# Batch 0's queries and keys loaded by runs of six rows, batch 2 turned on TensorE, batches 1 and 2 back to back

## The chip, the cores and the metric

The kernel runs on one core of one Trainium2 chip. The metric is device time in microseconds (us) of a whole execution, as the median of several. The span of a profile is about 1.8 us shorter than the time of the same execution, because it runs from the first to the last instruction.

## The reference, cut to what matters

Attention with 16 extra "beacon" keys in front of the causal ones, then a SwiGLU feed-forward block over all tokens.

```python
B, H, S, Nb, D = 8, 8, 576, 16, 64          # 4608 tokens of 512
k_all = concatenate([beacon_k, k], axis=2); v_all = concatenate([beacon_v, v], axis=2)
scores = (1 / sqrt(D)) * q @ k_all.T        # causal mask on the 576 ordinary keys
a = softmax(scores)
x = (a @ v_all).transpose(0, 2, 1, 3).reshape(B * S, H * D)
g = x @ w_gate                              # 512 -> 1536
out = (g * sigmoid(g) * (x @ w_val)) @ w_out
```

## The kernel before

Everything is kept in bf16, with f32 sums in PSUM. Per batch and pair of heads, the kernel multiplies turned (transposed) q by turned k (`S`, scores), takes exponentials on ScalarE, and multiplies by v (`P`). The result x is turned (`X`), and the feed-forward block eats it in chunks of 512 tokens: `G` is a gate unit of 8 products of 128x512 (1.73 us of TensorE at full clock), `F` one of its output products (0.22 us). The order of all these pieces is written by hand as a string, `plan`: each engine runs its part of the string strictly in order. So a piece whose data has not come yet stops TensorE, even where other work would be ready.

Before the scores, q and k must be turned so that D lies on the partitions. Batches 0 and 1 are turned on TensorE (`K`, `Q`: five transposes into a small PSUM bank, then a copy), later batches by DMA transposes (`t`). `l` is one load, issued by GpSimd, which also casts f32 to bf16. Of the other letters, `c` and `d` cast k and q of batch 0, `w` adds four spare turns without a result, `g` is a part of a gate unit, and a small `k`, `q` or `x` is the same turn, copied out by ScalarE.

```python
NPE = 2                                      # batches 0 and 1 are turned on TensorE
...
    def transpose_pair(dst, src, n, b, m, pool, tag, eng):
        t_ps = pool.tile([P, KPAD], BF16, name="t_ps", tag=tag)
        t, h = tiles(src[b % 2]), slice(2 * m, 2 * m + 2)
        while spare:                         # spare turns keep the clock up
            spare.pop()
            nc.tensor.transpose(t_ps[:, 0:P], below[:], ident[:])
        for c in range(NKT):
            r = P if c < 4 else 80
            nc.tensor.transpose(t_ps[:, P * c : P * c + r], t[0:r, c, h, :], ident[0:r, 0:r])
        o, i = dst[b % 2][:, m, 0 : 4 * P + n], t_ps[:, 0 : 4 * P + n]
        ...                                  # copied by ScalarE or VectorE
...
    start = v_loads(0, 0, 4) + q_loads(0, 4, H) + v_loads(0, 4, H)   # 17 issues
    for i in range(4):
        start += w_loads(i)                  # gate and value weights
    start += k_loads(1, 0, H) + q_loads(1, 0, H) + v_loads(1, 0, H)
...
    plan = [
        "lllllllllllllllllllllllllllllllwllllllllllloo",
        "dQwwwwcKdc", "SwwKcwwSwwwQ", "SKPcSQP", "SQKPXSP", "SPXSP",      # batch 0
        "gPgPgxXglgg", "ggGGGGGkKGGkQlGqkGG", "llqll",                   # gates; turns of batch 1
        "lSFFlFSFFFlqttltt", "ltllSFPFSPlllFltFFtFtSt", ...              # batch 1; DMA turns of batch 2
```

The softmax here doesn't subtract the row's maximum and nothing guards it: scores larger than these inputs give would overflow.

Of the kernel before, what the change touches and what calls it, by code (L numbers as in the profile page):

```python
# [8 lines left out]
ACT = mybir.ActivationFunctionType  # L9
ALU = mybir.AluOpType  # L10
BF16 = mybir.dt.bfloat16
FP32 = mybir.dt.float32
# [9 lines left out]
XWRAP, XSHIFT = 5 * TOK, 5 * TOK - P  # L22
XCOLS = XWRAP + P

NPE = 2

NHT = 2

# [23 lines left out]
def kernel(  # L52
# [37 lines left out]
    ident = static.tile([P, P], BF16, name="ident")  # L90
    below = static.tile([P, P], BF16, name="below")

    QK = NKT * H * D
    q32 = static.tile([P, QK // NPAIR * 2], FP32, name="q32")
    k32 = static.tile([P, QK], FP32, name="k32")
    qb = [static.tile([P, QK], BF16, name=f"qb{i}") for i in range(2)]
    kb = [static.tile([P, QK], BF16, name=f"kb{i}") for i in range(2)]
    vb = [static.tile([P, NKT, H, 68], BF16, name=f"vb{i}") for i in range(2)]
    qT = [static.tile([P, NPAIR, KPAD], BF16, name=f"qT{i}") for i in range(2)]
    kT = [static.tile([P, NPAIR, KPAD], BF16, name=f"kT{i}") for i in range(2)]  # L100
# [5 lines left out]


    def tiles(t):
        return t[:].rearrange("p (c h d) -> p c h d", c=NKT, d=D)

    def spans(eng, dst, src, b, h0, h1, c0, c1, r):

        for h in range(h0, h1):
            eng.dma_start(
                dst[:, c0:c1, h, 0:D],
                src[b, h, r : r + P * (c1 - c0), :].rearrange("(c p) d -> p c d", p=P),
            )

    loaded = {}

    def rows(eng, dst, src, b, h0, h1, c, p0, r, n):
# [3 lines left out]
        return eng.dma_start(  # L125
            dst[p0 : p0 + n, c, h0:h1, 0:D], src[b, h0:h1, r : r + n, :].rearrange("h j d -> j h d")
        )

    def load_q_f32(eng, b, h0, h1):
        spans(eng, tiles(q32), q, b, h0, h1, 0, 4, 0)  # L130
        rows(eng, tiles(q32), q, b, h0, h1, 4, 0, 512, 64)

    def load_k_f32(eng, b, h0, h1):
        d = tiles(k32)
        rows(eng, d, k, b, h0, h1, 0, NB, 0, P - NB)
        spans(eng, d, k, b, h0, h1, 1, 4, P - NB)
        rows(eng, d, k, b, h0, h1, 4, 0, 496, 80)

    def q_loads(b, h0, h1):
        d = tiles(qb[b % 2])  # L140
# [17 lines left out]
    def v_loads(b, h0, h1):  # L158
        return key_loads(nc.gpsimd, vb[b % 2], v, beacon_v, b, h0, h1)
# [16 lines left out]

    spare = []

    def cast_k(b, m):
        h = slice(2 * m, 2 * m + 2)  # L180
        nc.vector.tensor_copy(tiles(kb[b % 2])[:, :, h, :], tiles(k32)[:, :, h, :])

    def cast_q(b, m, eng):
        d, t, h = tiles(qb[b % 2]), tiles(q32), slice(2 * m, 2 * m + 2)
        for o, i in ((d[:, 0:4, h, :], t[:, 0:4, h, :]), (d[0:64, 4, h, :], t[0:64, 4, h, :])):
            if eng is nc.scalar:
                nc.scalar.activation(o, i, ACT.Copy)
            else:
                nc.vector.tensor_copy(o, i)

    def copy(eng, o, i):
        if eng is nc.scalar:
# [1 line left out]
        else:  # L194
            nc.vector.tensor_copy(o, i)

    def transpose_pair(dst, src, n, b, m, pool, tag, eng):
        t_ps = pool.tile([P, KPAD], BF16, name="t_ps", tag=tag)
        t, h = tiles(src[b % 2]), slice(2 * m, 2 * m + 2)

        while spare:
            spare.pop()
            nc.tensor.transpose(t_ps[:, 0:P], below[:], ident[:])
        for c in range(NKT):
            r = P if c < 4 else 80
            nc.tensor.transpose(t_ps[:, P * c : P * c + r], t[0:r, c, h, :], ident[0:r, 0:r])
        o, i = dst[b % 2][:, m, 0 : 4 * P + n], t_ps[:, 0 : 4 * P + n]
        if eng is nc.scalar:
            nc.scalar.activation(o, i, ACT.Copy)
        else:  # L210
            nc.vector.tensor_copy(o, i)

    def transpose_k(b, m, pool, tag, eng=None):
        transpose_pair(kT, kb, 80, b, m, pool, tag, eng)

    def transpose_q(b, m, pool, tag, eng=None):
        transpose_pair(qT, qb, 64, b, m, pool, tag, eng)

    def dma_transposes(b):
        def one(dst, src, c, n):  # L220
# [163 lines left out]


    nc.vector.memset(pt[1][:, 0, 0:TOK], 0.0)  # L386
    nc.vector.memset(tiles(k32)[64:P, 4, :, :], 0.0)
    rows(nc.gpsimd, tiles(k32), beacon_k, 0, 0, H, 0, 0, 0, NB)
    make_identity(nc, ident)

    nc.gpsimd.memset(below[:], 0.0)
# [16 lines left out]

    warm(18, TOK)
    for i in range(2):  # L410
        nc.vector.memset(tiles(qb[i])[64:96, 4, :, :], 0.0)
        nc.vector.memset(vb[i][:, :, :, D : D + 1], 1.0)
        nc.vector.memset(vb[i][64:P, 4, :, 0:D], 0.0)
        nc.vector.memset(kT[i][:, :, NB + S : KPAD], 0.0)
        nc.vector.memset(pt[i][:, :, 1664:P_W], 0.0)
    load_k_f32(nc.sync, 0, 0, 2)
    load_q_f32(nc.scalar, 0, 0, 2)
    load_q_f32(nc.scalar, 0, 2, 4)
    for m in range(1, NPAIR):
        load_k_f32(nc.sync, 0, 2 * m, 2 * m + 2)  # L420

    def kq_loads(b):

# [6 lines left out]



    done = dict.fromkeys("SPKQXgGFcdltwo", 0)
    first = [(0, 0, 1), (0, 1, 2), (1, 0, 1), (1, 1, 2), (0, 2, 3), (1, 2, 3), (0, 3, 4), (1, 3, 4)]
    parts = [(j, *part) for j in range(2) for part in first]
    units = [(j, f) for j in range(NCH) for f in range(2 if j < 2 else 0, NF)]
    def free(b, values=False):

        if b < 2 or values:
            return b < 2 or done["P"] >= 8 * (b - 1)  # L440
        return min(done["K"], done["Q"]) >= 4 * (b - 1) if b < 2 + NPE else done["t"] >= 10 * (b - 1 - NPE)

    def v_then(b, h0=0, h1=H):
        return [(load, b, True) for load in v_loads(b, h0, h1)]
# [1 line left out]
    def kq_then(b):  # L446
        return [(load, b, False) for load in kq_loads(b)]

    start = v_loads(0, 0, 4) + q_loads(0, 4, H) + v_loads(0, 4, H)
    for i in range(4):  # L450
        start += w_loads(i)
    start += k_loads(1, 0, H) + q_loads(1, 0, H) + v_loads(1, 0, H)
# [10 lines left out]
        return outp, "outp"  # L463

    def piece(kind):
        n = done[kind.upper()] if kind in "kqx" else done[kind]
        eng = nc.scalar if kind in "kqx" else nc.vector
        if kind == "S":
            b, m = n // 8, n % 8 // 2
            assert done["P"] >= 2 * (n // 2) - 2  # L470
            assert (min(done["K"], done["Q"]) > n // 2) if b < NPE else done["t"] >= 10 * (b - NPE + 1)
            scores(b, m, ("AB", "DC" if b == 0 else "CD")[n % 2])
        elif kind == "P":
            b, m = n // 8, n % 8 // 2
            assert done["S"] >= 2 * (n // 2 + 1)
            pv(b, m, n % 2, *small())
            if b >= NPE and n % 8 == 7:
                x_transpose(b)
        elif kind in "KkQq":
            turn = transpose_k if kind in "Kk" else transpose_q  # L480
            turn(n // 4, n % 4, *small(), eng)
        elif kind in "Xx":
            assert done["P"] >= 2 * (n + 1)
            x_transpose_pair(n // 4, n % 4, *small(), eng)
        elif kind == "g":
            j, f, k0, k1 = parts[n]
            assert done["X"] >= 4 * j + k1
            gv_mm(j, f, k0, k1)
            if k1 == KD:
                gv_act(j, f)  # L490
        elif kind == "G":
            j, f = units[n]
            assert j < NHT or done["F"] >= (j - NHT + 1) * 4 * NF
            assert done["g"] >= 8 * (j + 1) if j < 2 else done["P"] >= 8 * min(j + 1, B)
            gv_unit(j, f)
        elif kind == "F":
            if not projection:
                projection.extend(out_steps(n // (4 * NF), two_banks if done["P"] == 2 * NPAIR * B else one_bank))
            assert done["o"] == 2
            projection.pop(0)()  # L500
        elif kind == "o":
            load_wo(n)
        elif kind == "w":
            spare.extend(range(4))
        elif kind == "c":
            cast_k(0, n)
        elif kind == "d":
            cast_q(0, n, nc.scalar)
        elif kind == "l":
            load, b, values = loads[n]  # L510
            assert free(b, values)
            load()
        elif kind == "t":
            assert done["S"] >= 8 * (n // 10 + NPE - 1)
            turns[n]()
        done[kind.upper() if kind in "kqx" else kind] += 1

    one_bank = [(outp, "outp")]
    two_banks = [(outp, "outp"), (att, "att")]
    plan = [  # L520
        "lllllllllllllllllllllllllllllllwllllllllllloo",
        "dQwwwwcKdc",
        "SwwKcwwSwwwQ",
        "SKPcSQP",
        "SQKPXSP",
        "SPXSP",
        "gPgPgxXglgg",
        "ggGGGGGkKGGkQlGqkGG",
        "llqll",
        "lSFFlFSFFFlqttltt",  # L530
        "ltllSFPFSPlllFltFFtFtSt",
        "FXFPFSFP",
        "SXPFFSl",
        "llllll",
        "llPgtggPXlFFFlPggFFXgFgF",
        "glFSlSFllGFtttlS",
        "tltlllPGSFFlPGGlFFl",
        "ttttSlPtFFSlGPFlFl",
        "SlPFFFSPG",
        "SlPFFSFllFtPtGGFttt",  # L540
        "PSlllFFFFSlllPllGtGtFttt",
        "SFPFFSlGFFPGFG",
        "lFSPFFFFSFlFGllFlPGFGFlFSFF",
        "FllPFSFllFlPGGGFFFtltFFtt",
        "FlSPtFFFSlllPFFFGGFGFFFFFtttt",
        "SltlPFFFSllPFFFGGGFFFFFF",
        "SllPFFFSPFFFGGGFFFFFF",
        "SlllPFFFtSlllPFFGFGGFFFFFFtttt",
        "SlllPFFFSllPFFFGGGFFFFFFttttt",
        "SllPFFFSllPFFFGGGFFFFFF",  # L550
        "SllPFFFSPFFFGGGFFFFFF",
        "SPFFFSPFFFGGGFFFFFFttttt",
        "SPFFFSPFFFGGGFFFFFFttttt",
# [13 lines left out]
    for kind in "".join(plan).replace(" ", ""):  # L567
        piece(kind)
    del done["w"]
    assert done == dict(S=8 * B, P=8 * B, K=8, Q=8, X=8, g=16, G=len(units), F=4 * NF * NCH, c=4, d=2, o=2, l=len(loads), t=len(turns)), done  # L570


# [28 lines left out]
```

## Time and profile before

| | before |
|---|---|
| median time | 391.8 us |
| span of the profile | 390.7 us |
| TensorE busy | 368.9 us (94%) |
| first scores of batch 0 / 1 / 2 | 11.09 / 51.11 / 78.53 us |
| first full gate unit (batch 0 done) | 31.63 us |
| gate and value weights all landed | 34.9 us |

The row below is the DMA view of the kernel before from 2 to 36 us, 40 slices of 0.85 us: the busy share of the DMA engines in tenths (9 is 90% or more), and the GB/s written.

```profile
DMA  9999999999999999997999999999999999999999
GB/s 217 265 224 198 157 219 190 182 189 208 184 202 189 217 113 109 103 42 77 199 198 205 202 203 205 200 221 190 202 203 202 209 198 205 200 205 194 155 154 155
```

Fourteen slices (to 13.9 us) move batch 0's q, k and v at some 200 GB/s. Five slices of 42 to 113 follow, in which the weights have only just been issued (the first at 15.2 us). Then come the weights at 203, and at the end k of batch 1 at 155. The five weak slices are the only room in this row that an earlier issue could fill. They are not rest: the DMA engines are busy in them too, for 90% or more in four of the five, but little is written.

The last piece of weights, in the chain that ended last (issue, us to landing):

```profile
20.33 14.61 DMA wv<-in_moe_w_val_dram
```

### The profile page before, as it was taken

Reading aid. Unit: us, or ns where it says so; the run is one execution under the profiler, and the core shown is the slowest. Engines: PE = TensorE matmul, PEld = TensorE weight load, DVE = VectorE, ACT = ScalarE, POOL = GpSimd, SP = SyncE. Lnnn points to the kernel's source line nnn. Section 1 sums busy time; section 2 is a strip of 40 time slices with the busy share of each in tenths; the row PEclk is TensorE's granted clock in tenths of the full one; section 3 lists DMA queues with packets and bytes.
Section 4 is the critical chain, followed back from the end, with each engine's and each line's share of the span. In section 5 each row is a group of like instructions: output and inputs, shape, how many; then the busy total and the mean of one; then the engine's idle time right before and its main releaser. Section 6 shows DMA issues by size and latency. Waiting matters only on the chain.

```text
span 390.7 us, 7391 instructions
## 1 busy us (share of the span) xinstructions
PE 368.9 (94%) x2857; PEld 181.9 (47%) x2906; DVE 225.3 (58%) x413; ACT 172.4 (44%) x248; POOL 160.3 (41%) x275
## 2 busy tenths in 40 slices
PE   8899988679899999999999999999999999999995
PEld 3664555334454444444444444444445444444442
DVE  3567734625565566666666666666666636575652
ACT  2663577156665555555555555554552212222210
POOL 8946938577759566435653114311110000000000
PEclk9999999969999999999999999999999999999999
DMA  9999999999979999994998157813000211000012
GB/s 165 151 203 174 152 168 139 157 171 156 153 90 166 132 94 155 159 113 43 161 172 102 34 117 109 100 28 89 29 27 29 60 70 39 27 28 29 28 66 97
DMA packets 171364, 40.83 MB, mean 105 GB/s; under 512 B 161072, under 2 KB 166704, under 8 KB 171328
## 3 DMA queue, kind: packets, MB, share of 16 engines
q0 software_dynamic: 113600, 18.28, 68.8%
q1 hardware_dynamic: 55328, 21.48, 27.2%
q10 hardware_dynamic: 2400, 0.59, 0.8%
q8 instruction: 23, 0.38, 0.4%
q14 instruction: 13, 0.11, 0.1%
HBM read 38.27 MB, written 9.44 MB: 122 GB/s over the span
## 4 chain that ended last, share of the span: by engine, by line
PE 76%; DMA 9%; POOL 7%; DVE 3%; ACT 2%; issue 2%; SPq 1%; POOLq 0%; ACTq 0%
PE gv_ps L331 42%; PE o_ps L368 21%; PE pv_ps L286 6%; PE s_ps L241 5%; DMA wv<-in_moe_w_val_dram 4%; POOL vb L125 3%; DMA wo<-in_moe_w_out_dram 3%; DMA qT<-qb 2%; POOL qb L125 2%; ACT p L263 2%; ACT th L344 1%; POOL wg L164 1%; DVE u L346 1%; DVE hT L349 1%; SPq L222 1%
## 5 line engine op out<-in xcount | busy, mean ns | idle before, releaser
L344 ACT ACTIVATE th<-gv_ps 128x512 f32<-128x512 f32 x108 | 64.4, 597 | 164.1 <-PE gv_ps L331 163.4
L346 DVE SCALAR_TENSOR_TENSOR u<-th,gv_ps 128x512 f32<-128x512 f32 x108 | 74.3, 688 | 100.0 <-ACT th L344 99.7
L263 ACT ACTIVATE p<-s_ps 128x992 bf16<-128x992 f32 (+2 forms) x128 | 101.5, 863 | 29.5 <-PE s_ps L241 22.0
L331 PE MATMUL gv_ps<-xT,wg 128*128 128x512 bf16 x421 | 112.4, 381 | 2.0 <-ACT p L263 1.3
L331 PE MATMUL gv_ps<-xT,wv 128*128 128x512 bf16 x418 | 111.5, 381 | 0.8
L368 PE MATMUL o_ps<-wo,hT 128*128 128x512 bf16 x408 | 107.2, 379 | 3.9 <-DVE o_sb L377 1.9
L266 POOL TENSOR_SCALAR_AFFINE_SELECT p<-p 128x256 bf16<-128x256 bf16 (+2 forms) x120 | 44.2, 395 | 101.5 <-ACT p L263 101.4
L349 DVE SCALAR_TENSOR_TENSOR hT<-gv_ps,u 128x512 bf16<-128x512 f32 x108 | 74.7, 691 | 3.7
L331 PEld LDWEIGHTS <-wv 128*128 128x128 bf16 x432 | 42.5, 98 | 50.8 <-issue 1.3
L331 PEld LDWEIGHTS <-wg 128*128 128x128 bf16 x432 | 41.7, 98 | 49.2 <-issue 2.8
L368 PEld LDWEIGHTS <-hT 128*128 128x128 bf16 x432 | 39.2, 98 | 42.9 <-issue 3.7
L286 PE MATMUL pv_ps<-vb,p 128*128 128x65 bf16 x960 | 40.1, 193 | 3.2 <-DVE x L295 1.5
L286 PEld LDWEIGHTS <-p 128*128 128x128 bf16 x960 | 34.4, 97 | 18.2 <-issue 10.8
L241 PE MATMUL s_ps<-qT,kT 64*128 64x80 bf16 (+4 forms) x384 | 35.5, 286 | 5.3 <-DMA qT<-qb 3.1
L125 POOL DMA_DIRECT2D vb<-in_v_dram x45 | 37.0, 833 | 1.2 <-DMA qb<-in_q_dram 0.8
L125 POOL DMA_DIRECT2D qb<-in_q_dram x40 | 33.7, 848 | 8.1 <-DMA wo<-in_moe_w_out_dram 2.6
L125 POOL DMA_DIRECT2D kb<-in_k_dram x35 | 30.0, 858 | 14.4 <-DMA wv<-in_moe_w_val_dram 4.5
L295 DVE TENSOR_TENSOR x<-pv_ps,rec 128x320 bf16<-128x320 f32 x64 | 31.5, 492 | 2.4
L294 DVE RECIPROCAL rec<-pv_ps 128x5 f32<-128x5 f32 x64 | 12.3, 193 | 33.3 <-PE pv_ps L286 32.9
L377 DVE COPY o_sb<-o_ps 128x512 f32<-128x512 f32 x36 | 24.7, 687 | 7.8 <-PE o_ps L368 7.7
L241 PEld LDWEIGHTS <-kT 64*128 64x128 bf16 x384 | 13.2, 95 | 30.4 <-issue 22.3
L405 PE MATMUL idle_ps<-p 128*128 128x512 bf16 x18 | 6.8, 558 | 1.3 <-DVE p L386 1.3
(41 smaller groups left out, 76.2 us busy)
## 6 DMA issues: line engine op xcount, KB each, us to landing
out_dram<-o_sb SPq DMA_DIRECT2D x36, 256.0 KB, 2.3
qb<-in_q_dram POOLq DMA_DIRECT2D x28, 128.0 KB, 6.6
kb<-in_k_dram POOLq DMA_DIRECT2D x21, 128.0 KB, 8.9
vb<-in_v_dram POOLq DMA_DIRECT2D x21, 128.0 KB, 4.6
wg<-in_moe_w_gate_dram POOLq DMA_DIRECT2D x4, 384.0 KB, 9.2
wv<-in_moe_w_val_dram POOLq DMA_DIRECT2D x4, 384.0 KB, 10.9
wo<-in_moe_w_out_dram POOLq DMA_DIRECT2D x2, 768.0 KB, 10.7
kb<-in_k_dram POOLq DMA_DIRECT2D x7, 112.0 KB, 9.1
```

The lines of the kernel that those rows point to most:

```text
L125: return eng.dma_start(dst[p0 : p0 + n, c, h0:h1, 0:D], src[b, h0:h1, r : r + n, :].rearrange("h j d -> j h d"))
L241: nc.tensor.matmul(tiles[u][:, hh, col : col + n], lhsT=kT[b % 2][r, m, P * t : P * t + P], rhs=qT[b % 2][r, m, q0 : q0 + n],  start=not o ...
L263: nc.scalar.activation(p[:, :, c0 : c0 + w], tiles[u][:, :, 0:w], ACT.Exp, scale=0.125)
L266: nc.gpsimd.affine_select(out=ap, in_=ap, compare_op=ALU.is_ge, fill=0.0, base=d, pattern=[[0, 2], [1, n]], channel_multiplier=-1,)
L286: nc.tensor.matmul(o_ps[:, c, 0 : D + 1], lhsT=pt[m % 2][:, hh, col : col + P], rhs=vb[b % 2][:, t, h, 0 : D + 1], start=(t == 0), stop=(t ...
L295: nc.vector.tensor_tensor(out=xs[b][:, :, D * h : D * h + D], in0=o_ps[:, :, 0:D], in1=rec[:].to_broadcast([P, NKT, D]), op=ALU.mult,)
L331: nc.tensor.matmul(gvs[f][:, TOK * half : TOK * half + TOK], lhsT=w[:, kk, P * f : P * f + P], rhs=xT[:, kk, r : r + TOK], start=(kk == 0) ...
L344: nc.scalar.activation(th[:], ps[:, 0:TOK], ACT.Tanh, scale=0.5)
L346: nc.vector.scalar_tensor_tensor(out=u[:], in0=th[:], scalar=1.0, in1=ps[:, 0:TOK], op0=ALU.add, op1=ALU.mult)
L349: nc.vector.scalar_tensor_tensor(out=hTs[j][:, f, :], in0=ps[:, TOK:1024], scalar=0.5, in1=u[:], op0=ALU.mult, op1=ALU.mult)
L368: nc.tensor.matmul(st["o"][:], lhsT=hTs[j][:, f, P * i : P * i + P], rhs=wo[:, f, :], start=(f == 0), stop=(f == NF - 1),)
L377: nc.vector.tensor_copy(o_sb[:], st["o"][:])
```

## The change

There are three parts.

1. q and k of batch 0 come as runs of 6 rows per partition (96 partitions, rows of 1536 B, f32) on two hardware queues, eight loads in all. The casts and the copies out of PSUM put the order right. v of batch 0 takes 6 issues on GpSimd instead of 12, and five q issues go, so the weights can be issued sooner.
2. q and k of batch 2 are turned on TensorE too: a new piece `U` turns k and q of one pair into one two-bank PSUM slot. The ten DMA transposes of batch 2 go. Batch 1 uses `U` as well.
3. The order puts batches 1 and 2 back to back. Batch 1's first turn stands after one gate unit of chunk 0, not after five, and all of batch 2's turns stand inside batch 1's attention. The lines of `plan` for most later batches are arranged anew as well.

```diff
-NPE = 2
+NPE = 3
@@ loads of batch 0
+    def load_runs(eng, t, src, b, h0, h1):
+        eng.dma_start(
+            t[0:RP, ROWS * D * h0 : ROWS * D * h1].rearrange("p (h e) -> p h e", e=ROWS * D),
+            src[b, h0:h1].rearrange("h (p i) d -> p h (i d)", i=ROWS),
+        )
...
-    start = v_loads(0, 0, 4) + q_loads(0, 4, H) + v_loads(0, 4, H)
+    start = v_loads(0, 0, H)
@@ turns of batch 0: six (k: and one of the beacons), copied out at a stride
+        for i in range(ROWS):
+            col = P * (ROWS * m + i)
+            nc.tensor.transpose(
+                t_ps[:, NB + RP * i : NB + RP * i + RP], src[0][0:RP, col : col + P], ident[0:RP, 0:RP]
+            )
...
+            t_ps[:, NB : NB + S].rearrange("q (i p) -> q p i", i=ROWS),
@@ turns of batches 1 and 2
+    def transpose_both(b, m, engines):
+        t_ps = big.tile([P, 2, 1024], BF16, name="t2_ps", tag="big")
...
@@ plan
-        "dQwwwwcKdc",
-        "SwwKcwwSwwwQ",
-        "SKPcSQP",
+        "wwwwcdwKQwdc",
+        "SKcQSwwwdwwcKdS",
+        "PSQP",
...
-        "ggGGGGGkKGGkQlGqkGG",
-        "llqll",
-        "lSFFlFSFFFlqttltt",
-        "ltllSFPFSPlllFltFFtFtSt",
+        "gggGUGGGUGGGuGGuGl",
+        "lllllllllll",
+        "SFlFSFFUF",
+        "SPFSPUXFF",
+        "SPFFSPUXFF",
+        "SPFFSPUXFF",
...
```

## The prediction

> **What bounds the kernel now.** I read the page first, for the shares of the engines and the slices.
>
> ```profile
> PE 368.9 (94%) x2857; PEld 181.9 (47%) x2906; DVE 225.3 (58%) x413; ACT 172.4 (44%) x248; POOL 160.3 (41%) x275
> ...
> PE   8899988679899999999999999999999999999995
> ...
> PEclk9999999969999999999999999999999999999999
> ...
> DMA packets 171364, 40.83 MB, mean 105 GB/s; under 512 B 161072, under 2 KB 166704, under 8 KB 171328
> ```
>
> TensorE is busy for 94% of the span, and no other engine passes 58%. So a gain can only come from TensorE's idle time, its lost clock, or its work. The slices say where: the weak ones lie in the first third, with one slice at 5 to 7 tenths and one at a clock of 6 tenths near 70 to 90 us. Next I cut the span by stage with the busy-by-stretch view (length; busy PE, PEld, DVE, ACT, POOL; clock; DMA; GB/s).
>
> ```profile
> 7.87:31.60 23.73, 21.00 (x331) 15.30 (x332) 12.18 (x31) 15.19 (x23) 17.29 (x24) 1.00 1.47 180
> 31.60:50.75 19.15, 19.04 (x109) 9.44 (x110) 15.17 (x24) 8.46 (x15) 16.18 (x20) 1.00 1.92 159
> 50.75:68.00 17.25, 14.92 (x215) 9.38 (x217) 6.94 (x16) 13.39 (x18) 10.86 (x14) 1.00 2.21 155
> 68.00:76.10 8.10, 6.94 (x67) 3.64 (x63) 4.16 (x10) 1.65 (x4) 3.65 (x5) 1.00 1.65 166
> 76.10:81.60 5.50, 1.91 (x13) 0.80 (x14) 2.18 (x4) 2.53 (x4) 3.58 (x5) 0.72 1.96 159
> 81.60:100.00 18.40, 17.42 (x135) 7.67 (x136) 7.98 (x15) 10.61 (x16) 15.53 (x29) 0.90 1.97 157
> 100.00:140.00 40.00, 36.93 (x339) 18.44 (x344) 24.35 (x48) 23.34 (x33) 26.20 (x47) 1.00 1.55 130
> 140.00:280.00 140.00, 138.62 (x1110) 66.43 (x1129) 87.47 (x160) 71.28 (x101) 58.18 (x113) 1.00 0.90 101
> ```
>
> From 140 us on TensorE is 99% busy, and the change leaves that part alone. Between 50.75 and 140 us its idle time is 2.33 + 1.16 + 3.59 + 0.98 + 3.07 = 11.1 us. The timeline of TensorE shows the largest hole:
>
> ```profile
> 75.88 0.38 PE L368 MATMUL o_ps<-wo,hT 128*128 128x512 bf16 x1
> 78.53 0.59 PE L241 MATMUL s_ps<-qT,kT 64*128 64x496 bf16 x2 [2.28 <-DMA qT<-qb]
> 79.97 1.16 PE L241 MATMUL s_ps<-qT,kT 64*128 64x464 bf16 x10 [0.84 <-DMA qT<-qb]
> 81.64 1.86 PE L331 MATMUL gv_ps<-xT,wg 128*128 128x512 bf16 x4 [0.51 <-ACT p L263]
> 83.30 1.91 PE L331 MATMUL gv_ps<-xT,wv 128*128 128x512 bf16 x4
> 85.00 0.53 PE L368 MATMUL o_ps<-wo,hT 128*128 128x512 bf16 x1
> ...
> 86.94 1.02 PE L331 MATMUL gv_ps<-xT,wg 128*128 128x512 bf16 x4 [0.33 <-ACT p L263]
> ```
>
> The first scores of batch 2 wait for q turned by DMA (2.28 and 0.84 us). After that hole four gate products take 1.86 us, where the same four take 1.02 us at 86.94. The lost clock is worth 3.4 us at half rate, 1.7 us. So this hole costs some 3.6 + 1.7 = 5.3 us.
>
> **What the skill says.** "TensorE: Matmul & The Clock Gate", Part 1: the array falls to half its clock after an idle window of about 3.4 us and needs about as long busy to come back. The trace agrees: 3.6 us of idle time, then 3.4 us at half rate. "DMA: Bandwidth & Descriptors", Specifications: transfers under 512 B miss line rate. The trace is in keeping with it: 94% of the packets are under 512 B. While the weights stream (1536 B rows) the DMA writes about 205 GB/s of bf16, and under the head rows of 256 B some 155. "VectorE: DVE Perf Modes", Mode 2×_1P: two 16-bit elements per cycle only at step ±1. The trace fits: the copy of 576 contiguous bf16 from PSUM takes 0.46 us, that of 512 f32 takes 0.69.
>
> **The change, part by part.**
>
> Batch 0 by runs. Twelve SWDGE issues for v and five for q before the weights become six for v. In the GpSimd timeline they run from 3.1 to 15.2 us; six whole-head loads at 0.88 us or less are about 5 us, so the weights are issued from about 8 us, 7 us earlier. The bytes stay: q, k and v of batch 0 are 3.54 MB, the gate and value weights 6.29 MB. At the 410 GB/s of reads that the weights reach now (twice 205 written), 9.83 MB takes 24 us, so the last weights land near 26.5 us, not 20.3 + 14.6 = 35. All later loads are issued behind them on the same queue, so they move up by about 8.5 us. The first score hardly moves. The 18 warming products still hold TensorE until 7.9 us, 20 spare turns of 0.053 us still come before k, and k and q follow. Each VectorE copy out of PSUM now reads at a step of 96 elements, so I take 0.75 us for it instead of 0.46 (an estimate from the 0.69 us of 512 single elements), and k gets a second small copy for the beacons. ScalarE gets two more casts, about 0.8 us each, estimated from 0.62 us for 512; they fall in its gap of 1.46 us before the exponentials of pair 1. The stage lasts as long as now, or 0.3 us less.
>
> Batch 1 turned by pairs. The same 40 transposes, earlier, as the first turn stands after one gate unit (near 33 us) instead of after five. The last q of batch 1 was issued at 37.7 us and landed 4.8 us later, at 42.5; 8.5 us earlier is 34.0. So TensorE waits there up to 0.8 us.
>
> Batch 2 on TensorE. Ten DMA transposes go, and with them the wait and the dip: −5.3 us. In their place come 40 transposes. A set of five takes 0.26 us of TensorE's time now (16.41 to 16.67 us), so eight sets are 2.1 us, all on the bound engine. The new order asks for every k and q row of batch 2 at its first turn, in the second pair of batch 1. TensorE gets there at about 31.5 + 17.3 (ten units) + 2.1 (batch 1 turns) + 0.8 (wait) + 2.3 (two score steps, four output products) = 54.0 us. The last q of batch 2 lands now at 59.4 + 6.7 = 66.1 us. Minus 8.5, and minus some 1.8 because no DMA transpose runs beside it (loads land after 6.7 us there and 4.8 elsewhere), that is 55.8. So there is a wait of about 1.8 us, below what drops the clock.
>
> Batches 1 and 2 back to back. The rest of the idle time, 11.1 − 3.6 = 7.5 us, is short: one accumulator bank handed back by VectorE, p waiting for its mask, the output weights (0.8). The wait for the output weights goes. The others stay in kind: four exponentials of a pair take 3.1 us of ScalarE beside about 4.0 us of TensorE, and the turns take slots from the same three two-bank buffers. I leave 5.5 of the 7.5 us.
>
> Sum: −5.3 (hole and clock) − 2.0 (short waits) − 0.3 (batch 0) + 2.1 (transposes) + 0.3 (more, smaller turns in batch 0: two extra instructions per k set, one per q set, some 0.025 us each) + 0.8 + 1.8 (waits for loads) = −2.6 us. The author moved the turns up by the same 8 us that I give the loads, so I count the two load waits as half likely, which gives half of their 2.6 us back: −3.9 us. From 391.7 that makes 387.8 us.
>
> **Rivals.** First, the wait only moves: the loads of batch 2 come up by less than 8.5 us, because DMA bandwidth and not issue sets them, and TensorE stands at the first batch 2 turn for 5 us or more, at the cost of a clock dip again. For it: GpSimd sits waiting for the output weights at 50 to 57 us (2.6 and 3.7 us). Against it: between 13.5 and 18 us the DMA writes only 52 to 137 GB/s, room that earlier issue fills. This makes 391 to 394 us. Second, nearly all the idle time from 50 to 140 us goes, since batch 2 finishes before the gate work and later batches have slack everywhere: −5.3 − 6.0 + 2.4 − 0.3 = −9.2 us, 382.5 us. For it: the stretch from 140 us shows what a well-filled order reaches, 99%. Against it: with eight more two-bank slots to hand over, the dense attention stage is tighter than before. Third, batch 0 gets slower, by strided copies (some 3 us more VectorE work in 17 us, now 12.2 busy of 23.7) and two casts ahead of exponentials: up to +1.5 us.
>
> **Range and chances.** The main term and the transposes are fixed within 1 us; the load waits (0 to 6) and the short waits left over (2 to 7) are not. I take 383.8 to 392.0. Faster by 2% needs under 383.9 us, which only the second rival gives: 0.12. Slower by 2% needs a wait that nothing shows: 0.01.
>
> **What would show it.** Right: no DMA transpose feeds batch 2's scores, the clock row has no 6, the weights land near 26 us, scores of batch 0 start near 11 us, and TensorE's idle time between 50 and 140 us is 5 to 8 us. Wrong: a wait of over 3 us at the batch 2 turns for q or k loads (first rival), or under 3 us of idle time there (second), or exponentials of batch 0 that end well after 27 us (third).

## The result, and the profile after

The changed kernel takes 397.2 us (median of four, 397.05 to 397.53), the one before 391.8 (391.49 to 392.84). The ratio is 1.0134, with a 95% interval of 1.0114 to 1.0154. It is slower, and outside the predicted range. A ratio here is always the mean time of one kernel's fast runs over that of the other's of the same rounds, so it is not quite the ratio of the medians quoted.

The page of the changed kernel first: the engines' busy time, then the slices of TensorE and of its clock.

```profile
PE 373.3 (94%) x2905; PEld 185.4 (47%) x2954; DVE 230.8 (58%) x426; ACT 171.6 (43%) x244; POOL 152.7 (39%) x264
...
PE   7886999989988999999999999999999999999996
...
PEclk9899799999999999999999999999999999999999
```

The share of TensorE is the same 94%. The weak clock slice at 78 to 88 us is gone, but two others have come: an 8 at 10 to 20 us and a 7 at 40 to 50 us. The same stretches as before, in the busy-by-stretch view (length; busy PE, PEld, DVE, ACT, POOL; clock; DMA; GB/s):

```profile
7.87:31.60 23.73, 19.90 (x313) 14.65 (x315) 14.25 (x34) 15.52 (x20) 11.79 (x15) 0.93 1.53 201
31.60:50.75 19.15, 15.57 (x69) 6.83 (x70) 9.63 (x16) 3.78 (x7) 14.55 (x19) 0.82 1.83 151
50.75:68.00 17.25, 16.51 (x156) 9.32 (x156) 10.88 (x21) 10.42 (x15) 13.66 (x18) 1.00 2.08 147
68.00:76.10 8.10, 7.51 (x115) 4.61 (x116) 5.21 (x14) 5.05 (x8) 3.99 (x5) 1.00 1.81 134
76.10:81.60 5.50, 5.21 (x83) 3.32 (x83) 2.48 (x7) 4.25 (x6) 2.15 (x4) 1.00 1.51 103
81.60:100.00 18.40, 16.69 (x147) 8.16 (x147) 10.50 (x21) 9.45 (x15) 13.31 (x22) 1.00 1.28 121
100.00:140.00 40.00, 36.48 (x315) 17.71 (x317) 22.43 (x44) 22.82 (x32) 24.98 (x48) 1.00 1.20 114
```

From 50.75 to 140 us TensorE's idle time is 0.74 + 0.59 + 0.29 + 1.71 + 3.52 = 6.85 us (11.1 before), and the clock is full. The stretches hold other work now; counted over 88.9 us from batch 1's first scores in each kernel, the idle time is 6.96 us against 11.14. That is what the change set out to do. The loss is earlier: in 31.60 to 50.75 TensorE is busy 15.57 of 19.15 us at a clock of 0.82, where it was busy 19.04 at 1.00. The timeline of TensorE in that stretch shows why.

```profile
34.94 0.33 PE L226 MATMUL t_ps<-ident,kb 128*128 128x128 bf16 x3
35.88 0.23 PE L226 MATMUL t_ps<-ident,kb 128*128 128x128 bf16 x1 [0.60 <-DMA kb<-in_k_dram]
...
39.99 0.47 PE L226 MATMUL t_ps<-ident,qb 128*128 128x128 bf16 x2 [0.72 <-DMA qb<-in_q_dram]
40.39 1.89 PE L342 MATMUL gv_ps<-xT,wg 128*128 128x512 bf16 x4
...
45.21 1.03 PE L342 MATMUL gv_ps<-xT,wv 128*128 128x512 bf16 x4
```

Line 226 is the first turn of batch 1. TensorE gets there at 34.94 us and is through at 40.39: ten transposes in 5.45 us, with six waits of 0.39 to 0.72 us for k or q loads. In the kernel before, ten such turns take 0.53 us (44.38 to 44.91). So the wait costs 4.9 us against that kernel. (The later sets of ten in the changed kernel take 0.72 us; why is told under after_q80.) The next four gate products take 1.89 us instead of 1.03, and full rate is back only at 45.21. Three groups of four took 4.82 us there (40.39 to 45.21). At 0.86 us from start to start they would have taken 2.6, so the lost clock costs 2.2 us.

Where the time went, by milestones:

| | before | after | difference |
|---|---|---|---|
| first scores of batch 0 | 11.09 | 10.51 | −0.6 |
| first full gate unit | 31.63 | 33.08 | +1.45 |
| wait at batch 1's first turn | 0 | 4.9 | +4.9 |
| half clock after it | 0 | 2.2 | +2.2 |
| first scores of batch 1 | 51.11 | 60.43 | +9.3 |
| from there to the end of the span | 339.6 | 335.2 | −4.4 |
| span | 390.7 | 395.6 | +4.9 |

Of the +9.3 us, 1.45 + 4.9 + 2.2 = 8.55 are named. The other 0.75 is small; after_q80 below finds some 0.55 of it.

Why did the loads not come sooner? GpSimd's timeline of the changed kernel, its issues of the first, third and last piece of weights (start, length, what; in brackets the idle time before it and what ended it):

```profile
7.81 0.78 POOL L160 DMA_DIRECT2D wg<-in_moe_w_gate_dram  x1
...
11.90 0.74 POOL L160 DMA_DIRECT2D wg<-in_moe_w_gate_dram  x1 [2.54 <-DMA vb<-in_beacon_v_dram]
...
17.07 0.76 POOL L160 DMA_DIRECT2D wv<-in_moe_w_val_dram  x1
```

The first weights are issued at 7.8 us, as predicted. But GpSimd then stands still until earlier loads have landed, and the eighth piece goes out at 17.07 us, only 3.3 us sooner than before (20.33). The chain that ended last shows its flight, from issue to landing:

```profile
17.07 15.32 DMA wv<-in_moe_w_val_dram
```

That is 32.4 us, against 20.33 + 14.61 = 34.9 before: 2.5 us sooner, not 8.5. The GB/s row of the changed kernel over the same 2 to 36 us points to the cause:

```profile
GB/s 137 354 282 237 275 254 230 260 273 234 232 173 154 153 153 179 195 214 196 200 203 202 203 203 202 203 203 202 218 193 201 202 204 189 158 156 155 154 166 158
```

The weak slices are filled: none of the 40 writes under 137 GB/s. But batch 0's q and k now occupy eleven slices (to 11.4 us) at some 250 GB/s (the two hardware queues write 2.31 of the 2.37 MB moved in that time). Their f32 bytes are not cast on the way, so what is written is what is read, and all 2.36 MB count in full. Then v moves at 153, and only from about 15 us the weights at 203. Worked out by bytes *written*: 2.36 MB at 250 GB/s is 9.4 us, v's 0.59 MB at 153 is 3.9 us, and the weights' 3.15 MB of bf16 at 203 are 15.5 us. Together that is 28.8 us from about 2.5 us on, so 31.3; measured, 32.4. The rates are read from this very kernel, so the sum explains and does not forecast. In the kernel before, the five weak slices move on average 89 GB/s where 203 were possible, which is 4.25 us × (1 − 89/203) = 2.4 us of room. That room is just what was won.

### The profile page after: what moved, and what is told of

It reads as the page before. It is cut to its first block, busy times and chain, and to the rows that moved or that the text cites. A ratio compares the mean times of both kernels' runs of the same rounds, so it can differ in the third digit from the quotient of the medians.

```text
span 395.6 us, 7432 instructions
## 1 busy us (share of the span) xinstructions
PE 373.3 (94%) x2905; PEld 185.4 (47%) x2954; DVE 230.8 (58%) x426; ACT 171.6 (43%) x244; POOL 152.7 (39%) x264
## 3 DMA queue, kind: packets, MB, share of 16 engines
q10 hardware_dynamic: 832, 1.18, 1.2%
## 4 chain that ended last, share of the span: by engine, by line
PE 83%; DMA 8%; POOL 3%; DVE 2%; issue 2%; ACT 2%; POOLq 0%; ACTq 0%
PE gv_ps L342 46%; PE o_ps L379 22%; PE pv_ps L297 7%; PE s_ps L252 6%; DMA wv<-in_moe_w_val_dram 4%; DMA vb<-in_v_dram 2%; DMA qb<-in_q_dram 1%; ACT p L274 1%; POOL vb L131 1%; PE t_ps L226 1%; PE s_ps L264 1%; POOL qb L131 1%; DVE x L306 1%; ACT th L355 1%; DVE u L357 1%
## 5 line engine op out<-in xcount | busy, mean ns | idle before, releaser
L379 PE MATMUL o_ps<-wo,hT 128*128 128x512 bf16 x402 | 105.3, 379 | 3.3 <-DVE o_sb L388 1.9
L131 POOL DMA_DIRECT2D vb<-in_v_dram x40 | 33.9, 859 | 0.1
L131 POOL DMA_DIRECT2D qb<-in_q_dram x35 | 30.4, 870 | 6.6 <-PE gv_ps L342 3.6
L306 DVE TENSOR_TENSOR x<-pv_ps,rec 128x320 bf16<-128x320 f32 x64 | 31.5, 492 | 2.4
L187 DVE COPY kT<-t_ps 128x592 bf16<-128x592 bf16 (+2 forms) x14 | 6.1, 458 | 11.0 <-PE t_ps L201 6.3
## 6 DMA issues: line engine op xcount, KB each, us to landing
wo<-in_moe_w_out_dram POOLq DMA_DIRECT2D x2, 768.0 KB, 11.4
```

Of the source, the lines that this page charges most:

```text
L131: return eng.dma_start(dst[p0 : p0 + n, c, h0:h1, 0:D], src[b, h0:h1, r : r + n, :].rearrange("h j d -> j h d"))
L306: nc.vector.tensor_tensor(out=xs[b][:, :, D * h : D * h + D], in0=o_ps[:, :, 0:D], in1=rec[:].to_broadcast([P, NKT, D]), op=ALU.mult,)
L379: nc.tensor.matmul(st["o"][:], lhsT=hTs[j][:, f, P * i : P * i + P], rhs=wo[:, f, :], start=(f == 0), stop=(f == NF - 1),)
```

## The experiments

Thirteen kernels were run on chips beside the kernel before. The theory going in was this: the loss is a wait at batch 1's first turn, since the loads moved up by only 2.5 us, and the clock dip that follows it (load theory). The rivals were that the new stage of batches 1 and 2 is itself slower (crowding), that batch 0's new loads cost the time, and, within the load theory, whether bytes or GpSimd's issue order hold the loads back.

### u1_late: batch 1's first turn back behind five gate units

```diff
-        "gggGUGGGUGGGuGGuGl",
+        "gggGGGGGUGGUGGuGul",
```

> Only the order changes: the first turn of batch 1 stands after five gate units instead of one; batch 2's turns stay where they are. Theory A (the loads arrive when DMA bandwidth allows, about 40.0 us for the last q of batch 1 and 62.4 us for the last q of batch 2, and the order of TensorE runs ahead of both): the wait at batch 1's first turn (35 to 40 us in the changed kernel) and the half-rate clock after it go, TensorE reaches the first turn of batch 2 about 7 us earlier, near 56 us, and waits there until about 62 us with a new clock dip; the total stays within 2 us of the changed kernel's 397.2. Rival B (the wait at batch 1's first turn is the whole loss): about 7 us less, 390.

Measured: 396.31 us against 392.72, ratio 1.0099 (1.0058 to 1.0141). The wait at batch 1's turn is gone and its scores start at 53.3 us. The wait that I had predicted for batch 2's turn now appears (TensorE's timeline of this kernel):

```profile
59.04 0.23 PE L226 MATMUL t_ps<-ident,kb 128*128 128x128 bf16 x1 [1.10 <-DMA kb<-in_k_dram]
60.40 0.25 PE L226 MATMUL t_ps<-ident,kb 80*128 80x80 bf16 x1 [1.12 <-DMA kb<-in_k_dram]
...
61.78 0.98 PE L252 MATMUL s_ps<-qT,kT 64*128 64x496 bf16 x4 [0.47 <-issue]
```

The ten turns of batch 2's first pair take from 57.61 to 61.3 us, and four scores then take 0.98 instead of 0.58 us: half clock again. So in the changed kernel the first wait had only hidden a second one behind it. Removing one of them buys 0.9 us by the medians, 1.4 by the ratios.

### u_late: batch 2's turns behind batch 1's attention as well

```diff
-        "SFlFSFFUF",
-        "SPFSPUXFF",
-        "SPFFSPUXFF",
-        "SPFFSPUXFF",
+        "SFlFSFFF",
+        "SPFSPXFFF",
+        "SPFFSPXFFF",
+        "SPFFSPUXFFUF",
```

(and two more turns, loads and three output products moved along in the lines behind)

> Batch 1's turns after five gate units, and batch 2's turns after most of batch 1's attention, with output products of chunk 0 put in their place. Theory A: both waits for loads go, since the first turn of batch 2 falls near 64 us, after its last row at 62.4; 397.2 - 4.9 (wait) - 2.2 (clock) = about 390. Rival (batch 0 by runs, or crowding of the attention stage by turns in two-bank slots, is the cause of the loss): 394 or more, with no load wait in the trace.

Measured: 395.22 us against 392.72, ratio 1.0073 (1.0032 to 1.0114). My expectation was missed. No load wait is left in the trace, and batch 1's scores start at 53.90 us, 6.5 sooner than in the changed kernel. Yet batch 2's start at 76.70, only 1.8 sooner: batch 1's attention took 22.8 us instead of 18.1. It stands empty instead of waiting for loads, for slots (1.30 us behind a gate unit), for x (twice 0.81 us) and for an output tile:

```profile
69.04 0.95 PE L379 MATMUL o_ps<-wo,hT 128*128 128x512 bf16 x2 [0.93 <-DVE o_sb L388]
```

The clock is lost here too: two output products in 0.95 us instead of 0.59, and a granted clock of 0.79 from 68 to 76.1 us. So crowding is the wrong word, but the rival was partly right. The dense attention stage, bound by short waits, gives back 4.7 of the 6.5 us when the turns no longer fill it, and those need their loads.

### b0_only: the kernel before with part 1 of the change alone

```diff
 (diff against the kernel before: load_runs, cast, the turns of batch 0 and start = v_loads(0, 0, H)
  as in the change; NPE, the turns of batches 1 and 2 and the order from the gate units on as before)
-        "dQwwwwcKdc",
+        "wwwwcdwKQwdc",
```

> The kernel before with batch 0 by runs alone; batch 2 still turned by DMA, the order of before. Theory A: batch 0 ends about 1.4 us later than before (strided copies and two more casts), the weights and all loads behind them land about 2.5 us earlier, so the hole at batch 2's first scores (3.6 us idle and 1.7 us of clock) shrinks to nearly nothing: 388 to 390. If the loads did come 8.5 us earlier, as predicted, no hole at all would be left and the output weights would land near 48 us. Rival (runs only cost): 393.

Measured: 389.84 us against 392.72, ratio 0.9927 (0.9886 to 0.9968). The total is as expected. Batch 0 itself ends 3.4 us later than before (34.99 us) in the profiled run, where 1.4 was expected, with 1.18 us of waiting for the beacon keys, 1.33 for the strided copy of qT, and a clock of 0.86 in that stretch. But batch 2's first scores no longer wait for DMA:

```profile
78.97 0.38 PE L260 MATMUL s_ps<-qT,kT 64*128 64x496 bf16 x2
79.86 0.37 PE L260 MATMUL s_ps<-qT,kT 64*128 64x464 bf16 x2 [0.50 <-DVE hT L368]
```

So a load chain that is some 2.5 us sooner (taken over from the changed kernel; this trace does not show its landing), against an order that is now 3.4 us later, takes away the whole 5.3 us hole of the kernel before, without one transpose on TensorE. This answers the rival that batch 0's loads are to blame: they are the part of the change that gains.

### clock_fill: the changed kernel with 76 dummy transposes ahead of the first turn

```diff
-        "gggGUGGGUGGGuGGuGl",
+        "gggGwwwwwwwwwwwwwwwwwwwUGGGUGGGuGGuGl",
```

> The changed kernel with 76 dummy transposes (about 4.0 us of TensorE work without a result) just ahead of batch 1's first turn, where TensorE otherwise sits idle for 5 us. If the half-rate clock after the wait is a cost by itself, as its gate products of 1.68 instead of 0.86 us say, the wait stays as long in sum but the dip goes: about 2 us less than the changed kernel, 395. If the slow products are not due to the idle time, it stays at 397 or becomes longer.

Measured: 395.55 us against 392.72, ratio 1.0071 (1.0026 to 1.0116); the span is 393.9 instead of 395.6.

```profile
35.97 4.40 PE L224 MATMUL t_ps<-ident,below 128*128 128x128 bf16 x76
```

The dummies run from 35.97 to 40.2 us, just over the wait, and the granted clock from 31.6 to 50.75 us is 1.00. Batch 1's scores start at 58.75, 1.7 us sooner, although batch 0 ended 1.0 us later in this run. From the first product after the turns to those scores it is 17.8 us, against 20.0 in the changed kernel. So the dip is worth 2.2 us, as read from the products.

### fewer_bytes: only the first of four pairs of q and k of batch 0 loaded

This kernel computes the wrong thing on purpose (all pairs use pair 0). It still passed the comparison with the reference, which I take to come from the small q and k (an explanation that I did not test), so correctness says nothing for this run.

```diff
-            src[0:RP, cols].rearrange("p (h i d) -> p i h d", i=ROWS, h=2),
+            src[0:RP, 0 : 2 * ROWS * D].rearrange("p (h i d) -> p i h d", i=ROWS, h=2),
...
-    for m in range(NPAIR):
+    for m in range(1):
```

> Wrong on purpose: the changed kernel with only pair 0 of q and k of batch 0 loaded, and cast four times; everything else, the issues on GpSimd too, as in the changed kernel. 1.77 MB of its 2.36 MB of f32 are not fetched. Bandwidth theory: what is queued behind lands earlier by [...]about 5 us, so the last q of batch 1 lands near 35 us instead of 40, the wait at the first turn of batch 1 shrinks from about 5 us to 1 or less, no clock dip follows, and the time falls by 5 to 7 us, to 390 to 392. Issue theory (the order and the number of GpSimd's issues set the landing, as the prediction took it): no change, 397.

Measured: 393.02 us against 392.75, ratio 0.9994 (0.996 to 1.0029). Its last piece of weights in the chain that ended last:

```profile
13.00 16.36 DMA wv<-in_moe_w_val_dram
```

It lands at 29.4 us, 3.0 sooner than in the changed kernel. The last q of batch 1 is used at 37.2 instead of 40.0 us, the clock does not dip, and batch 1's scores start at 55.18. The issues run without a stop, from 7.78 to 13.00 us. The time is 4.2 us below the changed kernel's by the medians and 5.5 by the ratios. The theory that bytes do not matter is refuted, but the landing moves by 3 us and not by the 5 that I had expected. (At the 250 GB/s measured above, the 1.77 MB left out would even be worth 7.) The DMA moves only 30 to 163 GB/s from 4.5 to 11 us there, while v is issued and loaded: with the bytes gone, something else is the limit. That it is the issues is likely, but not shown.

### v_halves: v of batch 0 in 12 issues instead of 6, the same bytes

```diff
-    start = v_loads(0, 0, H)
+    start = v_loads(0, 0, 4) + v_loads(0, 4, H)
```

> The changed kernel with v of batch 0 issued by GpSimd in twelve pieces instead of six, so that GpSimd needs some 4 us longer before the weights; the bytes are the same. Bandwidth theory: the weights' third issue already waits until 11.9 us for v to land, so the last weights land within 1 us of the changed kernel's 32.4 and the time is within 1.5 us of its 397.2 (ratio to before 1.010 to 1.017). Issue theory, as the prediction took it: everything behind comes some 4 us later, the first wait grows to about 9 us, 401.

Measured: 399.88 us against 392.7, ratio 1.0185 (1.0156 to 1.0214). The extra issues themselves stand behind earlier loads (1.25, 1.09 and 1.47 us), the first weights go out at 15.35 us, and the last land 3.9 us later than in the changed kernel:

```profile
20.47 15.83 DMA wv<-in_moe_w_val_dram
```

The DMA runs at 45 to 80 GB/s from 13.9 to 18.2 us. So the issue order counts as well: 4 us of landing, and against the changed kernel 2.7 us of time by the medians, 2.0 by the ratios. My 1.5 us for the pure bandwidth theory was missed; the 4 us of landing that the issue theory gave was right. Taken together: whichever of the two is slower seems to set the pace. In the changed kernel as it stands the GB/s row has no gap, which speaks for the bytes there; fewer_bytes shows 3.0 us of them.

### b0_old: the changed kernel with batch 0 as before

```diff
+    load_k_f32(nc.sync, 0, 0, 2)
+    load_q_f32(nc.scalar, 0, 0, 2)
 ... (loads, casts, turns and order of batch 0 as in the kernel before)
-    start = v_loads(0, 0, H)
+    start = v_loads(0, 0, 4) + q_loads(0, 4, H) + v_loads(0, 4, H)
```

> The changed kernel with batch 0 loaded, cast and turned as in the kernel before; batches 1 and 2 as in the changed kernel. If runs move the loads up by 2.5 us and lengthen batch 0 by 1.4, then here the first turn of batch 1 is reached 1.4 us earlier, its last row lands 2.5 us later, and the wait there grows from about 5 to about 9 us: 398 to 400. If runs were the cause of the loss: 394 or less.

Measured: 400.00 us against 392.75, ratio 1.0183 (1.016 to 1.0206). As expected. TensorE reaches the turn at 33.4 us and leaves it at 42.8, with nine waits of 0.28 to 2.30 us and the dip after them. Its last piece of weights lands at 35.0 us, 2.6 later than in the changed kernel. Parts 2 and 3 alone lose 7 us, and part 1 wins back 2 (by the ratios) to 3 (by the medians) of these.

### b2_turn: b0_only with batch 2 turned on TensorE in the old places

```diff
-        "lSFFlFSFFFlqttltt",
-        "ltllSFPFSPlllFltFFtFtSt",
+        "lSFFlFSFFFlql",
+        "lllSFPFSPlllFlFFFS",
...
-        "llPgtggPXlFFFlPggFFXgFgF",
-        "glFSlSFllGFtttlS",
+        "llPgUggPXlFFFlPggFFXUgFgUF",
+        "gUlFSlSFllGFtttlS",
```

> Batch 0 by runs as in b0_only, the order of before kept (gate parts between batches 1 and 2), and batch 2 turned on TensorE in two-bank slots instead of by DMA, two to six us before its scores. b0_only has no load wait left before batch 2, so the turns can only add their 40 transposes, 2.1 us, less whatever they fill of holes: 390 to 392 beside b0_only's 389.8. Rival (taking ten DMA transposes away frees the queue and the DMA engines for later stages): 388 or less.

Measured: 391.69 us against 392.75, ratio 0.9974 (0.995 to 0.9998). As expected: 1.9 us over b0_only's median, which agrees with the 2.1 us worked out for eight sets of transposes on the bound engine. b0_only ran on another chip, so the ratios are the fairer comparison: 0.0047 of 392 us, 1.8 us. The two intervals overlap, so the size is rough. In the trace a set of ten turns takes 0.72 us (68.94 to 69.66, for one), so the four pairs hold TensorE for 2.9 us, not 2.1; some of that must have filled holes.

The first stretch of this run helps with batch 0 later (busy-by-stretch view, as above):

```profile
7.87:31.60 23.73, 20.39 (x336) 15.15 (x336) 14.22 (x34) 15.41 (x20) 11.62 (x16) 1.00 1.52 200
```

### b0_fast: b0_only with the start of batch 0 mended

```diff
+    beacons32 = static.tile([NB, H, D], FP32, name="beacons32")
-    nc.gpsimd.dma_start(beacons[:], beacon_k[0].rearrange("h j d -> j h d"))
+    nc.scalar.dma_start(beacons32[:], beacon_k[0].rearrange("h j d -> j h d"))
+    nc.vector.tensor_copy(beacons[:], beacons32[:])
-        "wwwwcdwKQwdc",
+        "wwwwcdwKqwdc",
```

> b0_only with batch 0's start mended: the beacons of k come first on ScalarE's queue in f32 and are cast by VectorE, so that the first turn doesn't wait for them (1.2 us in b0_only), and the first q is copied out of PSUM by ScalarE beside VectorE's copy of k (TensorE waited 1.3 us for the second copy). First scores near 9.5 us instead of 11.2, no clock loss in batch 0 (granted clock 0.86 there in b0_only), gate units from about 32 us instead of 35: 2 to 3 us less than b0_only, 387. If batch 0 is held by ScalarE's chain of exponentials and casts instead, less than 1 us.

Measured: 387.95 us against 392.75, ratio 0.990 (0.9841 to 0.9958); three runs lie at 386.95 to 388.01 and one at 391.44. This is what the start looks like in the changed kernel and in this one, the first scores of batch 0 in TensorE's timeline:

```profile
10.51 0.76 PE L252 MATMUL s_ps<-qT,kT 64*128 64x496 bf16 x4 [1.33 <-DVE qT L187]
```

```profile
10.50 0.58 PE L261 MATMUL s_ps<-qT,kT 64*128 64x496 bf16 x4 [0.74 <-ACT qT L183]
```

In the changed kernel VectorE copies k's beacons, k and q one after the other (0.83 and 0.75 us), and TensorE waits 1.33 us for the last. With q copied by ScalarE it waits 0.74 us and, in the profiled run, keeps its clock (1.00 in the stretch to 31.6 us). The first scores come 0.7 us sooner than in b0_only (11.22), where I had expected 1.7, and no sooner than in the changed kernel; but the stage ends at 31.7 us, as in the kernel before. This version beats both kernels.

### after_fast: the same mend in the changed kernel

```diff
-        "wwwwcdwKQwdc",
+        "wwwwcdwKqwdc",
 (and the beacons as in b0_fast)
```

> The changed kernel with the same mended start of batch 0 as b0_fast (beacons in f32 first, the first q copied by ScalarE). In b0_only that was worth 1.9 us. If the first turn of batch 1 is held by its loads, which don't move, it is worth nothing here: TensorE only comes earlier and waits longer, ratio to before 1.010 to 1.016. If batch 0's length is a cost by itself here too: 1.5 to 3 us less than the changed kernel, ratio 1.006 to 1.009.

Measured: 396.95 us against 392.7, ratio 1.0104 (1.0076 to 1.0132). Batch 0 ends 1.3 us sooner (31.80), but the last wait for q of batch 1 ends only 0.65 us sooner (39.34), and so batch 1's scores start at 59.87, 0.6 us sooner. The rest of the gain is waited away at the turn. This bears the load theory out: while the load is late, work that is done sooner is worth nothing.

### b0_fast2: b0_fast without 16 of the spare turns at the start

```diff
-        "wwwwcdwKqwdc",
+        "cdwKqwdc",
```

> b0_fast without the sixteen spare turns ahead of the first k (k's cast ends at 5.2 us and q's at 7.6 us there, the first turn stands at 9.0). First scores about 1 us earlier, 9.5 us; nothing behind waits for a load in b0_fast, so about 1 us less in all, 387. If the clock falls for want of the spare work, or ScalarE's chain sets batch 0, no gain or a loss.

Measured over five rounds: 388.43 us against 392.7, ratio 0.9893 (0.9853 to 0.9933). The first scores come at 9.70 us, 0.8 sooner, but the gate units start at 31.5, 0.1 to 0.2 us sooner. The expected microsecond was missed. The two versions are not told apart.

### after_q80 and b0_fast_q80: the last turn of each q set over 80 rows

This pair was for the 0.75 us that had no name. In the kernel before a set of five q turns takes 0.27 us to the next product; in the changed kernel it takes 0.45. First the kernel before, then the changed one, in TensorE's timeline:

```profile
44.64 0.42 PE L206 MATMUL t_ps<-ident,qb 128*128 128x128 bf16 x5
44.91 1.03 PE L331 MATMUL gv_ps<-xT,wg 128*128 128x512 bf16 x4
```

```profile
53.97 0.52 PE L226 MATMUL t_ps<-ident,qb 128*128 128x128 bf16 x5
54.42 1.04 PE L342 MATMUL gv_ps<-xT,wg 128*128 128x512 bf16 x4
```

The slot is another, and the last turn covers 64 rows where the kernel before took 80 (and left 16 columns uncopied). The edit takes 80 again:

```diff
+    nc.vector.memset(tiles(qb[1])[64:96, 4, :, :], 0.0)
-                r = P if c < 4 else 80 if src is kb else 64
+                r = P if c < 4 else 80
```

> The changed kernel, with the last turn of each q set of batches 1 and 2 over 80 rows (the spare 16 are zeros or old data, and their columns are not copied) instead of 64, as k's is and as the kernel before had it. In the changed kernel the q set takes 0.45 us from its start to the start of the next gate product, in the kernel before 0.27. Theory: the 64-row turn ahead of a 128-row product costs 0.18 us each. Then the q sets take 0.27 us, batch 1's first scores start about 0.55 us earlier (three sets outside the wait) and all of batch 2's sets gain up to 0.7 us where TensorE is the bound: time 0.5 to 1.2 us less than the changed kernel, a ratio of 1.0105 to 1.012. Rival: the 0.18 us belongs to the two-bank slot or the larger set; then the q sets stay at 0.45 us and the time at 397.

Measured over five rounds: 396.35 us against 392.84, ratio 1.0088 (1.0061 to 1.0115). The sets take 0.31 us (48.53 to 48.84 us, for one), so 0.14 of the 0.18 us is the 64-row turn. The ratio is below what I had expected (1.0105 to 1.012), with an interval that touches both that and the changed kernel's own. The medians differ by 0.84 us. So the shorter sets are shown, and the size in time only roughly: in the profiled run batch 1's first scores stand at 60.43 us again, because the half clock after the wait lasted longer (full rate at 46.55 us instead of 45.21), and from there to the end it takes 335.2 us as in the changed kernel. Three sets outside the wait at 0.18 us are 0.55 of the 0.75 us.

> The best version so far (0.990 and 387.95 us) with the same edit for the four q sets of batch 1, which take 0.45 us there though they are turned in a small one-bank slot. Theory of the 64-row turn: the sets take 0.27 us, 0.5 to 0.7 us less in all, about 387.3 us. Rival: no change in the sets and the time.

Measured over five rounds: 388.2 us against 392.84, ratio 0.9893 (0.9856 to 0.9931). The sets take 0.26 us (46.59 to 46.85), so the 64-row turn costs the same in the small slot. But the time is not told apart from b0_fast's. Its six runs range from 386.70 and 387.12 us at a mean clock of 1.00 to 390.65 and 390.67 at 0.994 and 0.990; the profiled one took 388.69 at 0.990. There the first stage had a clock of 0.86, after waits of 0.51 and 0.69 us for v, where b0_fast's had 1.00. The half clock in batch 0 comes and goes from run to run in these versions, and a spread of 4 us hides a gain of 0.7.

### What is common to all

From the first scores of batch 1 to the end of the span:

| kernel | first scores of batch 1 | from there to the end |
|---|---|---|
| before | 51.11 | 339.6 |
| u1_late | 53.31 | 341.3 |
| u_late | 53.90 | 341.0 |
| fewer_bytes | 55.18 | 336.0 |
| clock_fill | 58.75 | 335.2 |
| after_fast | 59.87 | 335.1 |
| after | 60.43 | 335.2 |
| after_q80 | 60.43 | 335.2 |
| b0_old | 63.16 | 335.2 |
| v_halves | 64.21 | 335.2 |

The back-to-back stage takes 335.2 us to the end whenever it starts late enough, at 58 us or after, with its loads on hand. Started at 53 or 54 us, it takes 341: in u1_late it waits for batch 2's loads, in u_late its order is another. So its gain of 4.4 us over the kernel before is real, but it rests on a start that is later than the gain pays for.

## Why the prediction was wrong, point by point

- **The step that failed**: "At the 410 GB/s of reads that the weights reach now …, 9.83 MB takes 24 us, so the last weights land near 26.5 us". They landed at 32.4. The 410 is a rate of loads that are cast, two bytes written for four read. q and k of batch 0 are not cast, so their bytes are read and written in full at about 250 GB/s, and v moves at 153 written. By bytes written the same sum gives 31.3 us. The kernel before had shown this in its row, at 200 GB/s written for the first 12 us. fewer_bytes shows that three quarters of these bytes cost 3.0 us of landing, and v_halves that six more issues cost 3.9.
- **"All later loads … move up by about 8.5 us"**: about 2.5. The last q of batch 1 was used at 40.0 us (34.0 predicted). TensorE reached its turn at 34.9 (33 predicted), so the wait was 4.9 us instead of 0.8.
- **"The author moved the turns up by the same 8 us … so I count the two load waits as half likely"**: this took the order of the code as evidence of timing, and none of the experiments bears it out. Both waits are there: the first in the changed kernel, the second in u1_late.
- **The clock dip**: I had put a dip under the first rival only and for batch 2. It came at batch 1: 2.2 us by the products, 1.6 us by the medians of the changed kernel and clock_fill, 2.5 by their ratios. The prediction took a wait of 1.8 us to be "below what drops the clock"; here no wait was over 0.72 us. It also read 3.6 us of idle time in the kernel before as one window of the skill's 3.4; the lines show three gaps, of 2.28, 0.84 and 0.51 us, so the trace did not bear that out.
- **The wait at batch 2's turns (1.8 us predicted)**: absent in the changed kernel, because TensorE was itself late. In u1_late the ten turns took 3.7 us, with a dip after.
- **Batch 0 (−0.3 us predicted)**: +1.45. This is the third rival, near its bound, but mostly by another mechanism. The sizes were right (strided copy 0.75 us as estimated, casts 0.84). The first scores even came 0.6 us sooner; 2.0 us were lost behind them. From the first scores to the first full gate unit it is 20.5 us in the kernel before, 22.6 in the changed kernel (clock of 0.56 from 10.5 to 14.4 us), and 21.2 in b2_turn, b0_fast and after_fast, whose clock stayed at 1.00. So 1.4 us are half clock and 0.7 the new work. What brings the dip is open: it comes behind short waits (0.63 us for the beacons, 1.33 for VectorE's three copies one after the other), but b2_turn had the wait of 1.33 us without a dip. b0_fast takes both waits down, and its clock was full in three of four runs.
- **Right**: no DMA wait and no dip at batch 2's scores (−5.3 us); idle time of 6.85 us between 50.75 and 140 us (5 to 8 predicted); first scores of batch 0 near 11 us. The terms for all after batch 1's first scores were −5.3 − 2.0 + 2.1 = −5.2 us, and −4.4 was measured, given the late start.
- **Right in total, by luck in part**: 2.1 us for the transposes of batch 2. b2_turn cost 1.8 to 1.9, but the eight sets hold TensorE for 2.9 us, because a q set takes 0.45 and not the 0.26 that the prediction read from a k set.
- **"The change leaves that part alone"** (from 140 us on): the order was changed there too, but it cost nothing. TensorE is idle for 6.6 us from 140 us to the end before, and for 6.5 us from 149.3 us to the end after.
- **The rivals**: the first, "the wait only moves", is what happened, one turn earlier than I had placed it, and with the cause that I gave: DMA bandwidth and not issue. Its 391 to 394 us were too low. The measured wait and dip alone make −5.2 + 4.9 + 2.2 = +1.9 us, 393.6, still in that range. Batch 0's 1.45, the 0.75 from the turns and the 0.8 us of missing gain bring it to +4.9, the difference of the spans.

What stays open: where the last 0.2 us before batch 1's first scores and the 0.8 us of missing gain behind them are (the eight longer sets of batch 2 add 0.8 us of TensorE's time, but shortening the q sets in after_q80 did not shorten this part in its profile); and whether an order exists in which TensorE reaches both turns just as their loads land and batch 1's attention is still filled. u_late was one try, and lost 4.7 of its 6.5 us.

## What to carry to other kernels

When a hand-written order is moved up against its loads, work out landing times from the bytes that the trace shows written, class by class (cast or not, long rows or short), and look for slices in which little is written: here 2.4 us of room was in them, and 2.5 were won. With one in-order engine a late load becomes a wait, and sometimes a clock dip on top (here, but not in fewer_bytes), and a wait removed may uncover the next one. Try the parts of a change apart: here one part alone, with a mended start, gains 1.0 to 1.1%, and the whole loses 1.3%.

## What the Trainium skill lacked or had wrong

- "TensorE: Matmul & The Clock Gate", Part 1, gives, in its table, an idle window of about 3.4 us for the fall to half clock; that frequent short idle times can bring it too, it says further down without a length. The runs show the fall without any unbroken idle time of that size: after six waits of 0.39 to 0.72 us with transposes between them (changed kernel, 34.94 to 40.39 us), and in u_late after waits of no more than 0.93 us each.
- The same page, Part 4, says that TensorE's transposes do not count as busy for the clock. In clock_fill 76 transposes and nothing else filled 4.4 us at 58 ns each, and the granted clock was 1.00, where it was 0.82 without them. The measurement decides for the transposes as this kernel issues them.
- The measured table of "DMA: Bandwidth & Descriptors", Bandwidth, gives rates by transfer size, and the text below it says why small descriptors are slow; neither has a rate for loads that are cast. In these runs the rate went by kind of load: about 250 GB/s for f32 rows of 1536 B that are not cast, 203 GB/s written (406 read) for weights cast to bf16, 153 to 155 written for head rows of 256 B cast to bf16. A table by bytes written would have helped with the step that failed.
- No page that I found says what a turn over 64 rows costs ahead of a product over 128: 0.14 to 0.19 us more than one over 80 rows (0.45 against 0.31 us a set in the two-bank slot, 0.45 against 0.26 in the small one).
- No page that I found says how long GpSimd stands before an issue until, by the profile, an earlier load has landed: 2.54 us at the third piece of weights here, and 0.62 to 2.2 us between the k loads behind the weights in v_halves and fewer_bytes.
